# Attention and a mixture of experts on one core: the split of the next block's first weight quarters is moved ahead of its rows' transpositions

## The chip, the core and the metric

The kernel runs on one core of a Trainium2 chip. The core has five engines, each with an instruction queue of its own: TensorE (PE in the profile, with its weight loads shown as PEld), VectorE (DVE), ScalarE (ACT), GpSimd (POOL) and SyncE (SP), which here mostly starts DMA transfers. Engines meet only through semaphores. The metric is device time of one execution in microseconds (us). Lower is better.

## The reference, cut to what matters

```python
# attention: B, H, S, D = 8, 8, 576, 64, rotary embedding on q and k
scores = scale * np.matmul(q_rot, k_rot.transpose(0, 1, 3, 2))
attn = softmax(scores)
x = np.matmul(attn, v)            # then reshaped to (4608, 512)
# mixture of experts: 8 experts, the best one for each token
logits = x @ w_gate + modality_bias[modality_id]
e_idx = np.argmax(logits, axis=1)
gate_w = softmax(logits)[arange, e_idx]
for e in range(8):
    mask = e_idx == e
    h = np.maximum(x[mask] @ w1[e], 0.0)              # 512 -> 1024
    out[mask] = gate_w[mask, None] * (h @ w2[e])      # 1024 -> 512
```

Every number is float32. The kernel keeps that precision by splitting an operand into a high part in a rounded format and a low part (the rest), and adding up three products: high by high, high by low and low by high.

## The kernel before

The first half of the program is attention, in 32 steps of one pair of heads each. As attention runs, tokens are routed: the rank of a token in its expert's list is worked out, and its number and gate weight are scattered into a table. The second half takes the table in blocks of 256 tokens that share one expert. The profiled execution runs 19 blocks: 8 whose plan is made after five of the eight batches, and 11 whose plan comes last.

A block `s` has these steps, written by the functions whose names begin with `m_`:

- `m_rows` (L736): GpSimd gathers the block's rows of x into a tile XG, 8 indirect transfers, two blocks ahead.
- `m_load1`, `m_load2` (L752, L757): SyncE loads the expert's two weight matrices in quarters of 512 KB into ST1 and ST2, one block ahead, and only where the expert changes from the block before.
- `m_split(0, g)`: quarter g of the first matrix: ScalarE copies ST1 to W1H (the high part, L274), then VectorE subtracts it from ST1 and writes W1L (the low part, L271).
- `m_tr` (L781) and `m_tre`: VectorE transposes the two halves of XG in place, in squares of 32; then for each half ScalarE writes the rows' high part and VectorE the low part. Both parts lie in a tile that the profile calls HL, so these rows read `HL<-XG`.
- `m_l1` (L801): TensorE's first product, 4 groups of 24 matmuls. The first three matmuls of a group take W1H with the rows' high part, W1H with the rows' low part, and W1L with the rows' high part.
- `m_l1e` (L809, L810): ScalarE and VectorE take a group's result out of PSUM with the relu, split in two parts.
- `m_split(1, g)`: the same split for quarter g of the second matrix (W2H, W2L).
- `m_l2` (L818, L821, L822): TensorE's second product for half t of the block, 24 matmuls; ScalarE scales the result into y, and GpSimd scatters y to the output.

`chain` writes this out for all blocks. While TensorE works on block `s`, the other engines prepare block `s + 1`: once the last group's relu of block `s` is written, they have the time of the two `m_l2` for that block's first split and transpositions.

Between these steps `one()` puts one step of a list that is left over from routing: 14 steps that route the last batch, 5 that scatter its table rows, and 7 rounds of the second plan's arithmetic. They are short instructions, mostly on VectorE: 6 steps in block 0, 10 in each of blocks 1 and 2, and none from block 3 on.

The order of the instructions on TensorE, ScalarE, VectorE and GpSimd is that of the program text, and each of these engines takes its instructions strictly in that order. SyncE's order in the expert part is chosen by a scheduler.

One thing differs in block 0: its first product and the first half of its second (`m_l2(0, 0)`, with its y on ScalarE) are written before `chain` begins, so y of that half stands ahead of everything that block 0 does for block 1.

Of the kernel before, what the change touches and what calls it, by code (L numbers as in the profile page):

```python
# [85 lines left out]
def tile_attention_moe(ctx: ExitStack, tc: tile.TileContext, qk, v, mod, wg, mb, w1, w2, rope, cf, ci, out):  # L86
# [619 lines left out]
    def m_plan(s):  # L706
        ph, i = slots[s]
        pl = PLB if ph else PLA
        ms[s] = dict(
            e=nc.sync.value_load(pl[0:1, 0, i:i + 1], min_val=0, max_val=E - 1),  # L710
            r=nc.sync.value_load(pl[0:1, 1, i:i + 1], min_val=0, max_val=(E + 1) * N - BLK),
            c=nc.sync.value_load(pl[0:1, 2, i:i + 1], min_val=0, max_val=1))

    def m_ix(s):
        d = ms[s]
        ix = d["ix"] = ixp.tile([P, 2, 2], I32, name="ix", tag="ix")
        i1 = nc.sync.dma_start(out=ix, in_=TAB[bass.ds(d["r"], BLK), :].rearrange("(p t) w -> p t w", t=2)).ins
        xi = d["xi"] = ixp.tile([P, 8, 2], I32, name="xi", tag="xi")
        i2 = nc.sync.dma_start(out=xi, in_=TAB[bass.ds(d["r"], BLK), :].rearrange("(q g) w -> q (g w)", g=8).unsqueeze(0).to_broadcast([4, 32, 16])).ins
        if not slots[s][0]:  # L720
            for i in (i1, i2):
                for b, x in placed:
                    if b >= NPL:
                        tc.declare_no_dep(i, x, reason="the first plan's blocks lie before the rows of later batches")
                    else:
                        tc.add_manual_dep(i, x.name, mybir.DependencyInfo(mybir.DependencyClass.Sync, mybir.DependencyReason.DATA),
                                          reason="the table's rows of the first plan's batches")
                taken.append(i)
# [16 lines left out]
    def m_rows(s):  # L745
        for t in range(2):
            for g in range(4):
                m_gather(s, t, g)

    def m_load1(s, g):  # L750
        d = ms[s]
        nc.sync.dma_start(out=ST1[:, :, g * 256:(g + 1) * 256],  # L752
                          in_=w1[bass.ds(d["e"], 1), :, g * 256:(g + 1) * 256].rearrange("o (c p) f -> p (o c) f", p=P), cond=d["c"])

    def m_load2(s, g):
        d = ms[s]
        nc.sync.dma_start(out=ST2[:, g * 2:g * 2 + 2, :],  # L757
                          in_=w2[bass.ds(d["e"], 1), g * 256:(g + 1) * 256, :].rearrange("o (c p) f -> p (o c) f", p=P), cond=d["c"])

    def m_hi(i, g):  # L760
        sl = slice(g * 256, (g + 1) * 256)
        if i == 0:
            acopy(W1[0][:, :, sl], ST1[:, :, sl])
        else:
            acopy(W2[0][:, g * 2:g * 2 + 2, :], ST2[:, g * 2:g * 2 + 2, :])

    def m_lo(i, g):
        sl = slice(g * 256, (g + 1) * 256)
        if i == 0:
            sub(W1[1][:, :, sl], ST1[:, :, sl], W1[0][:, :, sl].bitcast(F32))  # L770
        else:
            sl = slice(g * 2, g * 2 + 2)
            sub(W2[1][:, sl, :], ST2[:, sl, :], W2[0][:, sl, :].bitcast(F32))

    def m_split(i, g):
        m_hi(i, g)
        m_lo(i, g)

    def m_tr(s, t):
        x = XG[s % 2][:, t]  # L780
        nc.vector.transpose(x, x)  # L781

    def m_tre(s, t):
        x = XG[s % 2][:, t].rearrange("p g (c q) -> p c g q", q=32)
        oh, ol = (a[:, :, t * P:(t + 1) * P].rearrange("p c (q g) -> p c g q", g=4) for a in (XTH, XTL))
        acopy(oh, x)
        sub(ol, x, oh.bitcast(F32))
# [3 lines left out]
    def m_l1(s, g):  # L791
        d = ms[s]
        if g == 0:
            d["hh"], d["hl"] = HHL[s % 2]
        ps = bank("H").rearrange("p (c r) -> p c r", r=BLK)
        for i in range(2):
            f0 = (g * 2 + i) * P
            m = 0
            for c in range(4):
                for w, x in ((W1[0], XTH), (W1[0], XTL), (W1[1], XTH)):  # L800
                    l1_[s] = nc.tensor.matmul(ps[:, i, :], w[:, c, f0:f0 + P], x[:, c, :], start=(m == 0), stop=(m == 11)).ins  # L801
                    m += 1
        d["ps", g] = ps

    def m_l1e(s, g):
        d = ms[s]
        ps = d["ps", g]
        sl = slice(g * 2, g * 2 + 2)
        nc.scalar.activation(d["hh"][:, sl, :], ps, AF.Relu)  # L809
        nc.vector.scalar_tensor_tensor(d["hl"][:, sl, :], ps, 0.0, d["hh"][:, sl, :].bitcast(F32), op0=ALU.max, op1=ALU.subtract)  # L810

    def m_l2(s, t):
        d = ms[s]
        ps = bank("Y")
        m = 0
        for c in range(8):
            for hx, w in ((d["hh"], W2[0]), (d["hl"], W2[0]), (d["hh"], W2[1])):
                nc.tensor.matmul(ps, hx[:, c, t * P:(t + 1) * P], w[:, c, :], start=(m == 0), stop=(m == 23))  # L818
                m += 1
        y = yp.tile([P, DM], F32, name="y", tag="y")  # L820
        nc.scalar.activation(y, ps, AF.Copy, scale=d["ix"][:, t, 1:2].bitcast(F32))  # L821
        nc.gpsimd.indirect_dma_start(out=out, out_offset=bass.IndirectOffsetOnAxis(ap=d["ix"][:, t, 0:1], axis=0),  # L822
                                     in_=y, in_offset=None, bounds_check=N - 1, oob_is_err=False)
# [13 lines left out]
    def one():  # L837
        if late:
            f, *a = late.pop(0)
            f(*a)  # L840
# [20 lines left out]
    for n in range(NPAIR):  # L861
# [34 lines left out]
        if n % 4 == 3:  # L896
            K_("XO", xout, n // 4)
            g = route(n // 4)
            steps = [(next, g, None)] * (NRK - (n == z))
            scats = [(scatter, n // 4, j) for j in range(5)]  # L900
            if n == z:

                g = plan()
# [4 lines left out]
            if n == 4 * NPL - 1:  # L908
                g = plan0()
# [62 lines left out]
    def chain(lo, hi, begun):  # L972
        if not begun:
            for g in range(4):
                m_split(0, g)
            for t in range(2):
                m_tr(lo, t)
                m_tre(lo, t)
        for s in range(lo, hi):
            nxt = s + 1 < hi  # L980
            if nxt:
                if s + 2 < hi and (not begun or s > 0):
                    m_rows(s + 2)
                if s + 3 < hi and (not begun or s > 0):
                    if s + 3 not in ms:
                        m_plan(s + 3)
                    m_ix(s + 3)
                for g in range(4):
                    if not begun or s > 0:
                        m_load1(s + 1, g)  # L990
            if not begun or s > lo:
                for g in range(4):
                    m_split(1, g)
                    m_l1(s, g)
                    m_l1e(s, g)
                    one()
            if nxt:
                for t in range(2):
                    m_tr(s + 1, t)
                for t in range(2):  # L1000
                    m_tre(s + 1, t)
                    one()
                for g in range(4):
                    m_load2(s + 1, g)
            if not begun or s > lo:
                m_l2(s, 0)
            if nxt:
                m_split(0, 0)
                one()
                m_split(0, 1)  # L1010
                one()
            m_l2(s, 1)
            if nxt:
                m_split(0, 2)
                one()
                m_split(0, 3)
                one()

    ns = NA + NB_STATIC
    chain(0, ns, True)  # L1020
    order.close()
    tot = nc.values_load(TOT[0:1, 0:1], min_val=0, max_val=NB_MAX)  # L1022
    with tc.If(tot > NB_STATIC):
        prefetch(ns)
        chain(ns, NA + NB_MAX, False)
# [100 lines left out]
```

## Time and profile before

| | |
|---|---|
| median of 3 runs | 935.73 us (935.01 to 935.83) |
| the profiled execution | 935.48 us, of which the span from the first to the last instruction is 933.7 us |
| granted TensorE clock, mean | 0.998 |
| PE busy | 899.7 us, 96% of the span |
| DVE busy | 670.0 us, 72% |
| POOL busy | 664.9 us, 71% |
| ACT busy | 629.5 us, 67% |

The profile's busy times are sums over a program with two halves; the expert part takes the span from about 493 us to the end. "Releaser" or an arrow `<-` after an idle time names what the engine waited for. A row that ends in `x2` merges two instructions that followed each other, and its time is that of both. A block takes TensorE a little over 22 us.

### The profile page before, as it was taken

The page shows a single profiled execution, that of the slowest core. Times are in us where ns is not written, and L with a number is a line of the kernel's source. Part 1 is how long each engine was busy: PE and PEld are TensorE (multiplying, and loading weights), DVE is VectorE, ACT ScalarE, POOL GpSimd, SP SyncE. Part 2 cuts the span into 40 slices and gives each one's busy share as a digit, 9 for nine tenths or more (in the row PEclk, how much of TensorE's full clock was granted, in tenths as well). Part 3 has the DMA queues.
Part 4 walks back from the last instruction along what each step waited for, and adds up shares of the span by engine and source line. Part 5 has one row for each costly group of instructions (what it writes and reads, how often), then busy time and mean ns, then how long its engine had stood idle before and what let it go on. Part 6 is the DMA issues. An engine that isn't in the chain of part 4 may idle for free. (4 is left out here: it accounts for less than half of the span.)

```text
span 933.7 us, 24945 instructions
## 1 busy us (share of the span) xinstructions
PE 899.7 (96%) x9248; PEld 739.8 (79%) x9248; DVE 670.0 (72%) x1165; ACT 629.5 (67%) x1292; POOL 664.9 (71%) x498
## 2 busy tenths in 40 slices
PE   2999999999999999999999999999999999999996
PEld 2777777777777777777778888898889999999995
DVE  7577787777877778777886778666666666666661
ACT  2778787787878778787884665665555666665651
POOL 3988879898898988999933877776655666666400
PEclk9999999999999999999999999999999999999999
DMA  8856857677676775766752721117712511251100
GB/s 264 237 171 186 227 156 199 197 182 215 169 200 197 184 218 159 205 179 187 209 157 75 209 64 36 51 62 235 231 46 72 195 41 55 92 180 46 37 24 17
DMA packets 79292, 136.90 MB, mean 147 GB/s; under 512 B 28699, under 2 KB 50603, under 8 KB 78140
## 3 DMA queue, kind: packets, MB, share of 16 engines
q1 hardware_dynamic: 68460, 114.06, 43.5%
q0 software_dynamic: 9440, 19.46, 6.4%
q10 hardware_dynamic: 1264, 1.72, 0.6%
q8 instruction: 75, 1.23, 0.6%
q14 instruction: 53, 0.43, 0.2%
HBM read 140.59 MB, written 19.77 MB: 172 GB/s over the span
## 5 line engine op out<-in xcount | busy, mean ns | idle before, releaser
L330 ACT ACTIVATE P<-ps,mn 128x576 f32<-128x576 f32 x288 | 210.4, 737 | 91.2 <-DVE mn L323 91.0
L323 DVE TENSOR_REDUCE mn<-ps 128x1 f32<-128x576 f32 x288 | 204.0, 745 | 93.0 <-PE ps L314 52.7
L736 POOL DMA_INDIRECT XG<-X,iy x152 | 186.4, 1226 | 66.8 <-issue 49.7
L801 PE MATMUL psH<-HL,W1H 128*128 128x256 f32 x1152 | 204.1, 280 | 0.0
L314 PE MATMUL ps<-SW 64*128 64x288 f32 x960 | 166.8, 314 | 15.5 <-DMA SW<-HL 15.4
L801 PEld LDWEIGHTS psH<-HL,W1H 128*128 128x128 f32 x1152 | 177.3, 188 | 1.9 <-ACT W1H L274 0.5
L314 PE MATMUL ps<-HL 64*128 64x288 f32 x960 | 166.6, 313 | 0.9 <-ACT P L330 0.8
L801 PE MATMUL psH<-HL,W1L 128*128 128x256 f32 x576 | 161.6, 281 | 1.4 <-DVE W1L L271 1.4
L314 PEld LDWEIGHTS ps<-SW 64*128 64x128 f32 x960 | 134.9, 190 | 26.9 <-DMA SW<-HL 15.0
L314 PEld LDWEIGHTS ps<-HL 64*128 64x128 f32 x960 | 137.1, 190 | 22.2 <-issue 12.8
L271 DVE TENSOR_TENSOR W1L<-ST,W1H 128x1024 fp32r<-128x1024 f32 x76 | 90.2, 1223 | 80.2 <-ACT W1H L274 80.2
L392 PE MATMUL pa<-PH,V 128*64 128x320 f32 (+1 forms) x1024 | 138.3, 412 | 0.0
L822 POOL DMA_INDIRECT out_dram<-y,ix x38 | 40.5, 1067 | 126.1 <-ACT y L821 103.1
L818 PE MATMUL psY<-W2H,SW 128*128 128x512 f32 x304 | 121.2, 399 | 0.0
L818 PE MATMUL psY<-W2L,SW 128*128 128x512 f32 x304 | 119.8, 394 | 0.0
L336 PE MATMUL ps<-idf,P 64*128 64x64 f32 x2624 | 105.8, 230 | 7.3 <-ACT P L330 1.8
L336 PEld LDWEIGHTS ps<-idf,P 64*128 64x128 f32 x2624 | 92.9, 141 | 22.3 <-ACT PH L274 9.0
L801 PEld LDWEIGHTS psH<-HL,W1L 128*128 128x128 f32 x576 | 108.4, 188 | 1.8 <-DVE W1L L271 1.8
L291 POOL TENSOR_TENSOR HL<-ST,HL 128x1216 fp32r<-128x1216 f32 x31 | 86.1, 2776 | 32.7 <-ACT HL L274 32.5
L392 PEld LDWEIGHTS pa<-PH,V 128*64 128x64 f32 x1024 | 67.9, 136 | 48.4 <-issue 10.0
L368 DVE COPY PH<-ps 128x512 f32<-128x512 f32 (+1 forms) x160 | 96.1, 633 | 8.6 <-PE ps L336 8.0
L271 DVE TENSOR_TENSOR W2L<-ST,W2H 128x1024 fp32r<-128x1024 f32 x76 | 92.6, 1219 | 4.5 <-ACT W2H L274 4.4
(173 smaller groups left out, 1585.4 us busy)
## 6 DMA issues: line engine op xcount, KB each, us to landing
ST<-in_moe_w_dram SPq DMA_DIRECT2D x152, 512.0 KB
ST<-in_qk_dram SPq DMA_DIRECT2D x62, 608.0 KB
SW<-HL SPq DMA_DIRECT2D x124, 232.0 KB
V<-in_v_dram SPq DMA_DIRECT2D x32, 256.0 KB
X<-X SPq DMA_DIRECT2D x8, 1024.0 KB
XG<-X,iy POOLq DMA_INDIRECT x152, 3.2
V<-in_v_dram SPq DMA_DIRECT2D x64, 16.0 KB
X<-XT SPq DMA_DIRECT2D x16, 64.0 KB
```

The source lines that it names most:

```text
L271: nc.vector.tensor_tensor(o, a, b, op=ALU.subtract)
L291: e.tensor_tensor(d["HL"][:, 1, c], a, d["HL"][:, 0, c].bitcast(F32), op=ALU.subtract)
L314: free(nc.tensor.matmul(ps[:, g, 0:288], t[:, wq, q0:q0 + P], t[:, wk, k0:k0 + 288], start=(m == 0), stop=(m == len(L) - 1)), seen)
L323: lastmin[d["ring", u]] = nc.vector.tensor_reduce(mn, d["S", u][:, :, 0:288], op=ALU.min, axis=AX.XY).ins
L330: nc.scalar.activation(p.rearrange("p (a b) -> p a b", a=2), ps[:, :, 0:288], AF.Exp, bias=d.pop(("m", u)), scale=-1.0, accum_out=d["sum"] ...
L336: free(nc.tensor.transpose(ps[0][:, g, c:c + 64], src[r, k0:k0 + P], idf[r, r]), ps[1])
L368: mine.append((nc.vector.tensor_copy if g else acopy)(o, i).ins)
L392: i = nc.tensor.matmul(pa[hh * 64:hh * 64 + 64, 0:c1 - c0], d["V"][:, hh, kt, :], r, start=(kt == 0), stop=(kt == 4))
L736: inst = nc.gpsimd.indirect_dma_start(out=XG[s % 2][:, t, g, :], out_offset=None, in_=X.rearrange("n (i f) -> (n i) f", f=P)[0:rows], in_o ...
L801: l1_[s] = nc.tensor.matmul(ps[:, i, :], w[:, c, f0:f0 + P], x[:, c, :], start=(m == 0), stop=(m == 11)).ins
L818: nc.tensor.matmul(ps, hx[:, c, t * P:(t + 1) * P], w[:, c, :], start=(m == 0), stop=(m == 23))
L822: nc.gpsimd.indirect_dma_start(out=out, out_offset=bass.IndirectOffsetOnAxis(ap=d["ix"][:, t, 0:1], axis=0), in_=y, in_offset=None, bounds ...
```

## The change

In `chain`, the two calls of `m_split(0, 0)` and `m_split(0, 1)` for block `s + 1`, each with a `one()` behind it, move from between the two `m_l2` to ahead of the two `m_tr`.

```diff
             if nxt:
+                for g in range(2):
+                    m_split(0, g)
+                    one()
                 for t in range(2):
                     m_tr(s + 1, t)
                 for t in range(2):
                     m_tre(s + 1, t)
                     one()
                 for g in range(4):
                     m_load2(s + 1, g)
             if not begun or s > lo:
                 m_l2(s, 0)
-            if nxt:
-                m_split(0, 0)
-                one()
-                m_split(0, 1)
-                one()
             m_l2(s, 1)
             if nxt:
                 m_split(0, 2)
```

Nothing is added or removed, and TensorE's and GpSimd's orders stay as they are. On VectorE, at the end of block 0 (the `XG` and `W1L` here belong to block 1; `lg` to `vm` are the left-over routing steps), the order before is:

```order
L525 TENSOR_REDUCE of<-rk 128x5
L781 STREAM_TRANSPOSE XG_76<-XG_76 128x512 x2
L271 TENSOR_TENSOR HL_81<-XG_76,HL_81 128x4x4x32 x2
L481 TENSOR_REDUCE lg<-G 128x40
L483 TENSOR_REDUCE mx<-lg 128x5
L271 TENSOR_TENSOR W1L<-ST_73,W1H 128x4x256
L486 TENSOR_TENSOR dl<-lg,mx 128x40
L488 TENSOR_SCALAR vv<-dl 128x40
L489 TENSOR_TENSOR vv<-vv,CF 128x40
L271 TENSOR_TENSOR W1L<-ST_73,W1H 128x4x256
```

and in the changed kernel:

```order
L525 TENSOR_REDUCE of<-rk 128x5
L271 TENSOR_TENSOR W1L<-ST_73,W1H 128x4x256 x2
L481 TENSOR_REDUCE lg<-G 128x40
L483 TENSOR_REDUCE mx<-lg 128x5
L781 STREAM_TRANSPOSE XG_76<-XG_76 128x512 x2
L271 TENSOR_TENSOR HL_81<-XG_76,HL_81 128x4x4x32
L486 TENSOR_TENSOR dl<-lg,mx 128x40
L488 TENSOR_SCALAR vv<-dl 128x40
L489 TENSOR_TENSOR vv<-vv,CF 128x40
L271 TENSOR_TENSOR HL_81<-XG_76,HL_81 128x4x4x32
```

The two weight subtractions moved to the front, and the routing steps `lg` and `mx`, which follow the second of them, now stand ahead of the transpositions; `dl` to the second `vv` stand between the two row subtractions.

On ScalarE at the same place, from block 0's first y on, the order before is:

```order
L821 ACTIVATE y<-psY,ix 128x512
L274 ACTIVATE HL_81<-XG_76 128x4x4x32
L274 ACTIVATE G<-XT 64x2x4x4 x2
L274 ACTIVATE HL_81<-XG_76 128x4x4x32
L274 ACTIVATE W1H<-ST_73 128x4x256 x2
```

and in the changed kernel:

```order
L821 ACTIVATE y<-psY,ix 128x512
L274 ACTIVATE W1H<-ST_73 128x4x256
L274 ACTIVATE G<-XT 64x2x4x4 x2
L274 ACTIVATE W1H<-ST_73 128x4x256
L274 ACTIVATE HL_81<-XG_76 128x4x4x32 x2
```

The weight copies changed places with the row copies. The first y stands ahead of both.

On VectorE at the end of block 1 (the `XG` and `W1L` here belong to block 2), the order before is:

```order
L810 SCALAR_TENSOR_TENSOR HL_82<-psH,SW_84 128x512
L781 STREAM_TRANSPOSE XG_75<-XG_75 128x512 x2
L271 TENSOR_TENSOR HL_81<-XG_75,HL_81 128x4x4x32
L520 TENSOR_TENSOR rk<-rk,OH 128x40
L271 TENSOR_TENSOR HL_81<-XG_75,HL_81 128x4x4x32
L522 RECIPROCAL VAL<-ee 128x5
L271 TENSOR_TENSOR W1L<-ST_73,W1H 128x4x256
```

and in the changed kernel:

```order
L810 SCALAR_TENSOR_TENSOR HL_82<-psH,SW_84 128x512
L271 TENSOR_TENSOR W1L<-ST_73,W1H 128x4x256
L520 TENSOR_TENSOR rk<-rk,OH 128x40
L271 TENSOR_TENSOR W1L<-ST_73,W1H 128x4x256
L522 RECIPROCAL VAL<-ee 128x5
L781 STREAM_TRANSPOSE XG_75<-XG_75 128x512 x2
L271 TENSOR_TENSOR HL_81<-XG_75,HL_81 128x4x4x32
```

Here too the weight subtractions moved ahead of the transpositions, with two short routing steps between them.

SyncE's order changes as well, in blocks 3 and 4 only: the loads of the first two W1 quarters for a later block move ahead of a run of reads of the second plan, and the loads of the other two quarters behind more of these reads than before.

## Rows read from the trace of the kernel before

**Rows 1.** Busy time of the engines in one block's stretch (TensorE first).

```profile
587.00:610.00 23.00, 23.00 (x148) 20.74 (x147) 16.24 (x17) 13.51 (x16) 16.78 (x15) 1.00 0.17 52
```

**Rows 2.** Waits of TensorE: total us, times, longest.

```profile
PE psH L801 <- DVE W1L L271: 1.4, 2, 0.8
```

**Rows 3.** Timeline of TensorE, start of block 1: start us, us, instruction, idle before.

```profile
518.09 0.40 PE L801 MATMUL psH<-HL,W1H 128*128 128x256 f32 x2
519.15 0.39 PE L801 MATMUL psH<-HL,W1L 128*128 128x256 f32 x1 [0.67 <-DVE W1L L271]
```

**Rows 4.** Timeline of TensorE, end of block 1 and start of block 2.

```profile
541.70 0.40 PE L818 MATMUL psY<-W2L,SW 128*128 128x512 f32 x1
542.13 0.51 PE L801 MATMUL psH<-HL,W1H 128*128 128x256 f32 x2
543.39 0.39 PE L801 MATMUL psH<-HL,W1L 128*128 128x256 f32 x1 [0.75 <-DVE W1L L271]
```

**Rows 5.** Timeline of TensorE, start of block 3.

```profile
565.71 0.40 PE L801 MATMUL psH<-HL,W1H 128*128 128x256 f32 x2
565.95 0.28 PE L801 MATMUL psH<-HL,W1L 128*128 128x256 f32 x1
```

**Rows 6.** Timeline of ScalarE, end of block 0.

```profile
512.69 0.69 ACT L821 ACTIVATE y<-psY,ix 128x512 f32<-128x512 f32 x1 [3.64 <-PE psY L818]
513.27 1.11 ACT L274 ACTIVATE HL<-XG 128x512 fp32r<-128x512 f32 x1
514.18 0.47 ACT L274 ACTIVATE G<-XT 64x32 f32<-64x32 f32 x2
514.67 1.14 ACT L274 ACTIVATE HL<-XG 128x512 fp32r<-128x512 f32 x1
```

**Rows 7.** Timeline of VectorE, end of block 0.

```profile
510.17 1.29 DVE L781 STREAM_TRANSPOSE XG<-XG 128x512 f32<-128x512 f32 x2
...
516.86 0.87 DVE L481 TENSOR_REDUCE lg<-G 128x40 f32<-128x360 f32 x1
...
517.88 1.21 DVE L271 TENSOR_TENSOR W1L<-ST,W1H 128x1024 fp32r<-128x1024 f32 x1
519.01 0.19 DVE L486 TENSOR_TENSOR dl<-lg,mx 128x40 f32<-128x40 f32 x1
...
519.57 1.22 DVE L271 TENSOR_TENSOR W1L<-ST,W1H 128x1024 fp32r<-128x1024 f32 x1
```

**Rows 8.** Timeline of all engines, end of a later block and start of the next.

```profile
689.44 0.60 ACT L809 ACTIVATE SW<-psH 128x512 fp32r<-128x512 f32 x1 [1.27 <-PE psH L801]
...
690.68 1.29 DVE L781 STREAM_TRANSPOSE XG<-XG 128x512 f32<-128x512 f32 x2
...
692.62 2.09 DVE L271 TENSOR_TENSOR HL<-XG,HL 128x512 fp32r<-128x512 f32 x2 [0.65 <-ACT HL L274]
...
695.67 2.00 ACT L274 ACTIVATE W1H<-ST 128x1024 fp32r<-128x1024 f32 x2
...
696.75 2.36 DVE L271 TENSOR_TENSOR W1L<-ST,W1H 128x1024 fp32r<-128x1024 f32 x2 [2.04 <-ACT W1H L274]
...
700.43 0.40 PE L801 MATMUL psH<-HL,W1H 128*128 128x256 f32 x2
```

**Rows 9.** Timeline of VectorE, end of block 1.

```profile
538.76 0.71 DVE L781 STREAM_TRANSPOSE XG<-XG 128x512 f32<-128x512 f32 x1 [4.11 <-DMA XG<-X,iy]
...
542.11 1.23 DVE L271 TENSOR_TENSOR W1L<-ST,W1H 128x1024 fp32r<-128x1024 f32 x1 [0.19 <-ACT W1H L274]
```

**Rows 10.** Timeline of VectorE, end of block 2.

```profile
556.71 1.30 DVE L781 STREAM_TRANSPOSE XG<-XG 128x512 f32<-128x512 f32 x2
...
564.23 1.22 DVE L271 TENSOR_TENSOR W1L<-ST,W1H 128x1024 fp32r<-128x1024 f32 x1
```

**Rows 11.** Timeline of TensorE, attention's first steps.

```profile
26.78 0.44 PE L314 MATMUL ps<-HL 64*128 64x288 f32 x1
...
35.31 0.29 PE L314 MATMUL ps<-SW 64*128 64x288 f32 x1
```

## The prediction

> **What bounds the kernel now.** I read first the busy times by stretch, then TensorE's waits, then TensorE's timeline at each place where one block ends and the next begins, and last what VectorE and ScalarE do there. In a stretch of one block TensorE is busy for all of 23.00 us, VectorE for 16.24 and ScalarE for 13.51 [rows 1]. So the expert part is TensorE's, and the other engines count only where they hand it something late. In the expert part TensorE's list has one wait, for W1L, 1.4 us in two places [rows 2]. Both are at starts of a block's first product: block 1 [rows 3] and block 2 [rows 4]. Each is a little more in clock time than the row's idle figure. The third matmul of a block normally starts 0.24 us after the first (565.95 - 565.71, [rows 5]). In block 1 it starts at 519.15, with the first at 518.09, so it is 519.15 - 518.33 = 0.8 us late. In block 2 the last matmul of the block before starts at 541.70; matmuls of that product follow each other at about 0.23, so the first could start at 541.93 and the third at 542.17; it starts at 543.39, 1.2 us late. These 2.0 us are all that an earlier W1L can win.
>
> **What the change does in a block without routing steps.** No instruction is added, so only the order counts: what TensorE needs at the start of the next block is W1 quarter 0 and the rows' two parts, and the rows now come last. Before, the last relu starts at 689.44, the rows are complete at 692.62 + 2.09 = 694.7, and W1L quarter 0 is there half-way through the pair of 2.36 that starts at 696.75, at about 698.0; TensorE begins at 700.43 and takes W1L as its third matmul [rows 8]. After: the weight copy can start when the relu ends, 690.04; its subtraction follows 696.75 - 695.67 = 1.08 later, at 691.1; the pair takes about 2.3, to 693.4; the row subtractions begin 692.62 - 690.68 = 1.94 after the transpositions begin, at 695.3, and end 2.09 later at 697.4. TensorE wants the rows' low part with its second matmul, at 700.55. The slack is 3.1 us where it was 2.7 for W1L: nothing changes there. y of the first half stands behind the row copies in either order and its tile has room, so it is hidden. The quarters' loads on SyncE are released about 5 us earlier, and they are used a block later, so that is hidden too. In blocks 3 and 4 SyncE's reads of the second plan stand ahead of other loads; behind them come the second matrix's loads, which wait in any case for this block's subtractions, so I cost it at nothing, and a load late by more than the 3 us slack would be what it costs if that cover is gone.
>
> **End of block 0: a new wait.** Here ScalarE stands on y of the first half until 512.69 and is free at 513.27 [rows 6]. Before, VectorE's transpositions ran inside that wait, at 510.17 [rows 7], and ScalarE's first work behind y was the rows. Now VectorE's first instruction is a weight subtraction, which must wait for a weight copy behind that y, and everything else queues behind it:
> - weight copy 0 starts at 513.27, its subtraction 1.08 later (the step from rows 8) at 514.35;
> - the two G copies hold ScalarE 514.67 - 514.18 = 0.49, after a copy's 0.91 to 0.95 (513.27 to 514.18), so weight copy 1 starts at 514.7 and its subtraction at 515.8. A subtraction holds VectorE 519.01 - 517.88 = 1.13, to 516.9;
> - `lg` and `mx` take 517.88 - 516.86 = 1.02, to 517.95;
> - the transpositions start there, the first row subtraction 1.94 later (rows 8) at 519.9, and it holds VectorE about 1.0 (half of 2.09), to 520.9;
> - `dl` and the two `vv` take 519.57 - 519.01 = 0.56, to 521.45;
> - the second row subtraction takes 1.1, to 522.5.
>
> So TensorE's second matmul of block 1 starts at about 522.6 and the third at 522.7 in place of 519.15 [rows 3]. That is 3.6 us later than before, with the old wait for W1L inside it. What TensorE then does is the same, and all of block 1's other work follows TensorE's relu steps, so the rest moves by 3.6 as a whole.
>
> **End of block 1: an old wait goes.** In the new time TensorE is ready for block 2 at 541.93 + 3.6 = 545.5. What holds the rows before is a gather that GpSimd issued earlier: the second transposition waits 4.11 for it, to 538.76, and the W1L subtraction that stands behind the rows starts at 542.11 [rows 9], so by the gather the rows are complete at about 542. By the other bound, the chain of a plain block, they are complete 697.4 - 689.44 = 8.0 after the last relu starts, and TensorE comes 700.43 - 689.44 = 11.0 after it [rows 8]; two short routing steps in between take some 0.5. The slack is over 2 us on either count, and W1L was done long before. So the 1.2 us of lateness at 543.39 goes.
>
> **End of block 2: close.** VectorE's work from the transpositions at 556.71 to the end of the second weight subtraction, 564.23 + 1.22 = 565.45, is one set of instructions, and the change permutes it: the row subtraction now ends it [rows 10]. TensorE wants that at 565.71 + 0.12 = 565.83 [rows 5]. I take 0; the bounds are 0 and 0.5 lost, if an extra handover falls in between.
>
> **The sum.** 3.6 - 1.2 = 2.4 us on the profiled execution's 935.48, so 937.9; the median of the runs shown is 0.25 higher, so 938.1. I count a difference of over 0.2% (1.9 us) as what a measurement of this kernel can tell from no change; the forecast is just beyond it.
>
> **What no row prices: TensorE's clock after the new stop.** TensorE would stand still from about 518.2 to 522.6, but for a matmul or two. Its stops in the expert part before are under 1 us [rows 3, 4], and the block behind them still runs at 0.28 a matmul [rows 5]. In attention's start the 288-column matmuls take 0.44 at 26.78 and 0.29 at 35.31 [rows 11]: the slow one of its two levels and the fast one (1.2 and 2.4 GHz), although the profile's granted clock reads 1.00 in both. So a stop could cost from 0 to, if the slow level lasted those 8.5 us at half rate, 4.3 us. I take 0 for the likeliest, because every stop seen after the start kept the fast level, and keep both ends.
> The Trainium skill, "TensorE: Matmul & The Clock Gate", section "Why this matters for your kernels", says that an idle gap of TensorE between bursts puts its clock back to half rate. No stop in this trace is long enough to show it; by that rule the clock rival below would be the result.
>
> **The rivals.**
> 1. The clock falls at the new stop. For it: the stop is several times any other in this part, and the slow level exists in this trace. Against it: no fall is seen after the start. With 2 us, the middle of 0 and 4.3, it gives 940.1.
> 2. The old waits go and no new one comes, which is faster: 935.73 - 2.0 = 933.7. The place is the same, end of block 0. It decides at 518.2, when TensorE wants the rows' low part: if the rows are complete by then, the change wins. For it: in each plain block the order has 3 us of slack. Against it: y at 512.69 stands ahead of all, and the steps behind it add up to 522.5, 4.3 us too late.
> 3. The new wait is real but small, or more comes back later, so that no change can be told: the wait would have to be under 3.1 us in place of 3.6 (1.9 + 1.2), as if the routing steps between the rows cost VectorE nothing (1.02 + 0.56 less gives a sum of 0.8). That gives 936.5. It is also where a change that does little ends up.
>
> **How the numbers follow.** The forecast has 0.57, with a range of its own of 937.3 to 938.9 (0.3 less or 0.5 more of VectorE's handovers, 0.5 at block 2). The clock has 0.20, the small wait 0.16, the faster rival 0.07. Of the forecast's chance about 0.50 lies beyond the 1.9 us and 0.07 within it; with the clock that is 0.70 slower, with the small wait 0.23 the same, and 0.07 faster. The range from 935.6 to 941.2 leaves out the faster rival and the upper half of the clock's price, together under 0.2.
>
> **What would show it.** In the changed kernel's timeline the transpositions for block 1 should start near 518 and not 510, the second row subtraction should end near 522.5, and TensorE's row at the start of block 1 should show a wait of some 1.7 to 4.4 us, named for the rows (HL) and not for W1L. No wait for W1L should be left. At the start of block 2 the wait should be gone, and the shift of TensorE against before should be 2.4 us from there to the end. A matmul of block 1 at twice the 0.12 step would show the clock. If the shift at block 1 is under 3 us, my steps on VectorE are wrong; if it changes after block 3, it is SyncE's order or a gather that I costed at nothing.

## The result, and the profile after

The changed kernel takes 940.19 us (median of 6 runs, 938.34 to 941.30), the kernel before 935.37 us (6 runs). The ratio is 1.0042, 95% interval 1.0027 to 1.0057: slower by 3.9 us (2.5 to 5.3) by the ratio; the two medians lie 4.8 apart. Run again, on one chip beside other kernels, it took 939.00 us against 935.71, ratio 1.0042 again (1.0026 to 1.0058). The forecast was 938.1 and slower.

The profiled execution took 940.92 us with a span of 939.0, which is 5.3 more than before. Of this only a part belongs to the change: block 0's last matmul already starts 1.7 us later (519.57 against 517.86), behind an attention part whose instructions are the same in both. Over the twelve profiled executions of this study that start lies anywhere between 516.7 and 520.0. So below I compare traces by the **tail**: from the start of block 0's last matmul to the end of the span. It is 933.7 - 517.86 = 415.8 before and 939.0 - 519.57 = 419.4 after, 3.6 more.

TensorE's list of waits in the changed kernel has no W1L any more, and two waits for the rows, in place of [rows 2] (columns: total us, times, longest):

```profile
PE psH L801 <- ACT HL L274: 2.7, 1, 2.7
PE psH L801 <- DVE HL L271: 1.4, 1, 1.4
```

Its timeline from the end of block 0 on answers to [rows 3]:

```profile
519.57 0.40 PE L818 MATMUL psY<-W2L,SW 128*128 128x512 f32 x1
522.62 0.39 PE L801 MATMUL psH<-HL,W1H 128*128 128x256 f32 x1 [2.65 <-ACT HL L274]
524.42 0.58 PE L801 MATMUL psH<-HL,W1H 128*128 128x256 f32 x1 [1.42 <-DVE HL L271]
524.80 0.41 PE L801 MATMUL psH<-HL,W1L 128*128 128x256 f32 x1
...
525.44 0.41 PE L801 MATMUL psH<-HL,W1L 128*128 128x256 f32 x1
...
527.36 0.41 PE L801 MATMUL psH<-HL,W1L 128*128 128x256 f32 x1
...
527.90 0.28 PE L801 MATMUL psH<-HL,W1L 128*128 128x256 f32 x1
...
528.26 0.28 PE L801 MATMUL psH<-HL,W1L 128*128 128x256 f32 x1
```

Two things stand in these rows. TensorE stops for 2.65 us, does one matmul, and stops for 1.42 more. And behind the second stop three matmuls take 0.64 (525.44 - 524.80) until about 527.6, and 0.36 from there on (528.26 - 527.90): the slow one of TensorE's two levels, 1.2 GHz, for some 3 us. The busy times by stretch show that too. The sixth figure behind the stretch's own length (the counts in brackets left out) is the granted clock, 1.00 before (first row) and 0.93 in the changed kernel:

```profile
517.00:541.00 24.00, 23.33 (x152) 20.85 (x151) 16.72 (x29) 12.27 (x17) 19.32 (x18) 1.00 0.79 212
517.00:541.00 24.00, 19.93 (x130) 18.14 (x129) 18.49 (x31) 13.23 (x18) 19.62 (x18) 0.93 0.72 189
```

ScalarE at the end of block 0, which answers to [rows 6], has the weights where the rows were, behind the same y:

```profile
514.40 0.69 ACT L821 ACTIVATE y<-psY,ix 128x512 f32<-128x512 f32 x1 [3.66 <-PE psY L818]
514.98 1.05 ACT L274 ACTIVATE W1H<-ST 128x1024 fp32r<-128x1024 f32 x1
...
520.52 2.04 ACT L274 ACTIVATE HL<-XG 128x512 fp32r<-128x512 f32 x2 [3.05 <-issue]
```

And VectorE, which answers to [rows 7]:

```profile
516.07 1.23 DVE L271 TENSOR_TENSOR W1L<-ST,W1H 128x1024 fp32r<-128x1024 f32 x1 [4.13 <-ACT W1H L274]
517.50 1.22 DVE L271 TENSOR_TENSOR W1L<-ST,W1H 128x1024 fp32r<-128x1024 f32 x1 [0.21 <-ACT W1H L274]
...
519.73 1.30 DVE L781 STREAM_TRANSPOSE XG<-XG 128x512 f32<-128x512 f32 x2
521.66 1.11 DVE L271 TENSOR_TENSOR HL<-XG,HL 128x512 fp32r<-128x512 f32 x1 [0.63 <-ACT HL L274]
...
523.27 1.10 DVE L271 TENSOR_TENSOR HL<-XG,HL 128x512 fp32r<-128x512 f32 x1
```

VectorE idles 4.13 us for the weight copy behind y; before, it transposed in that time. The transpositions start at 519.73, which is 518.0 in before's time, and the second row subtraction ends at 524.37, or 522.7. At the start of block 2 there is no wait any more, against [rows 4]; the last row is the start of block 3, against [rows 5]:

```profile
548.51 0.39 PE L818 MATMUL psY<-W2L,SW 128*128 128x512 f32 x1
548.74 0.40 PE L801 MATMUL psH<-HL,W1H 128*128 128x256 f32 x2
548.98 0.28 PE L801 MATMUL psH<-HL,W1L 128*128 128x256 f32 x1
...
571.20 0.40 PE L801 MATMUL psH<-HL,W1H 128*128 128x256 f32 x2
```

The account by the trace has three parts:

- The stop: the second matmul starts 4.85 us behind block 0's last one (524.42 - 519.57), so at the fast level the third would start at 4.97; before it started at 1.29 (519.15 - 517.86). That is 3.7 more, with the old wait of block 1 inside it.
- The slow stretch: from the third matmul to the start of block 2 it is 23.94 us (548.74 - 524.80), where before it was 22.78 to the time at which block 2 could have started (541.93 - 519.15), and the step from the second matmul to the third is 0.38 in place of 0.12. That is 1.4 more.
- The old wait of block 2: 1.2 less.

That sums to 3.9. Block 3 starts 51.6 us behind block 0's last matmul (571.20 - 519.57), against 47.9 before (565.71 - 517.86), which is 3.8 more. From there to the end it is 367.8 us, against 368.0 before, so nothing more is lost in the later blocks.

### The profile page after: what moved, and what is told of

It reads as the page before. It is cut to its first block, busy times and chain, and to the rows that moved or that the text cites. A ratio compares the mean times of both kernels' runs of the same rounds, so it can differ in the third digit from the quotient of the medians.

```text
span 939.0 us, 24928 instructions
## 1 busy us (share of the span) xinstructions
PE 900.9 (96%) x9248; PEld 741.4 (79%) x9248; DVE 670.1 (71%) x1165; ACT 625.0 (67%) x1292; POOL 669.6 (71%) x498
## 5 line engine op out<-in xcount | busy, mean ns | idle before, releaser
L736 POOL DMA_INDIRECT XG<-X,iy x152 | 182.9, 1203 | 66.7 <-issue 50.0
L822 POOL DMA_INDIRECT out_dram<-y,ix x38 | 46.6, 1226 | 125.4 <-ACT y L821 110.3
```

The source lines that it names most:

```text
L736: inst = nc.gpsimd.indirect_dma_start(out=XG[s % 2][:, t, g, :], out_offset=None, in_=X.rearrange("n (i f) -> (n i) f", f=P)[0:rows], in_o ...
```

## The experiments

The theory (A): the whole loss is made at one place, the end of block 0. There block 0's first y stands on ScalarE ahead of the weight copies; VectorE, whose queue now begins with a weight subtraction, idles behind it, and the rows come too late. The stop also drops TensorE's clock. The rivals: later blocks or SyncE's new order cost something; the weight split ahead of the rows costs by itself; the slow stretch has a cause other than the stop.

| kernel | median us | before beside it | ratio (95% interval) | tail against before |
|---|---|---|---|---|
| the change | 940.19 | 935.37 | 1.0042 (1.0027 to 1.0057) | +3.6 |
| the change again | 939.00 | 935.71 | 1.0042 (1.0026 to 1.0058) | +3.7 |
| in block 0 alone | 941.00 | 935.90 | 1.0056 (1.0037 to 1.0075) | +3.9 |
| in all blocks but 0 | 934.47 | 935.90 | 0.9981 (0.9968 to 0.9993) | -1.4 |
| routing steps behind the rows | 937.65 | 935.90 | 1.0021 (1.0006 to 1.0035) | 0.0 |
| first y behind the rows | 933.19 | 935.90 | 0.9973 (0.9962 to 0.9984) | -2.1 |
| the stop filled | 937.99 | 935.71 | 1.0023 (1.0011 to 1.0035) | +2.3 |
| before, first y behind the rows | 937.30 | 935.71 | 1.0021 (1.0001 to 1.0040) | +0.6 |

**In block 0 alone.** The new order is used at `s == 0`, the old one behind it.

```diff
-                for g in range(2):
-                    m_split(0, g)
-                    one()
+                if s == 0:
+                    for g in range(2):
+                        m_split(0, g)
+                        one()
...
+            if nxt and not (s == 0):
+                for g in range(2):
+                    m_split(0, g)
+                    one()
             m_l2(s, 1)
```

> The change is made at the end of block 0 alone; blocks 1 to 17 keep the old order. Theory A (the whole loss is made at the end of block 0: a new stop of TensorE of about 4.4 us, a stretch at its slow clock behind it, and the old wait of block 2 gone because TensorE comes later): the same as the whole change, 4 to 5 us slower than before, and TensorE's row at the start of block 1 waits for HL as there. Theory B (a part of the loss comes from the later blocks, by SyncE's new order or by transfers): at least 1 us less loss than the whole change, 2 to 3.5 us slower than before.

It is 1.0056 times before, no better than the whole change, with the same stop and the same slow matmuls:

```profile
518.23 0.40 PE L818 MATMUL psY<-W2L,SW 128*128 128x512 f32 x1
521.26 0.39 PE L801 MATMUL psH<-HL,W1H 128*128 128x256 f32 x1 [2.64 <-ACT HL L274]
523.09 0.43 PE L801 MATMUL psH<-HL,W1H 128*128 128x256 f32 x1 [1.44 <-DVE HL L271]
523.32 0.41 PE L801 MATMUL psH<-HL,W1L 128*128 128x256 f32 x1
```

So theory A holds for the loss. It tells one thing more: in this kernel block 2 has the old order, and its wait for W1L is gone too. TensorE's lateness alone is enough to make it go.

**In all blocks but 0.** The condition is turned round, `s > 0`.

> The change is made at the ends of blocks 1 to 17; block 0 keeps the old order. Theory A: the 0.8 us of lateness at block 1 stays, the 1.2 us at block 2 go, no new wait: 1.2 us faster than before (0.7 to 1.5). Theory B: 1 to 2 us slower than before, with a wait or a shift of TensorE behind block 2.

It is faster than before, ratio 0.9981 with an interval that leaves out 1. The wait at block 1 stays, that at block 2 is gone with TensorE on time:

```profile
517.04 0.40 PE L801 MATMUL psH<-HL,W1H 128*128 128x256 f32 x2
518.18 0.38 PE L801 MATMUL psH<-HL,W1L 128*128 128x256 f32 x1 [0.74 <-DVE W1L L271]
...
540.91 0.40 PE L801 MATMUL psH<-HL,W1H 128*128 128x256 f32 x2
541.14 0.28 PE L801 MATMUL psH<-HL,W1L 128*128 128x256 f32 x1
```

So the moved split alone is enough too to make the wait at block 2 go; in the whole change both hold. In these blocks the change does what it can: 1.2 us were forecast, the tail is 1.4 shorter. No loss comes from the later blocks.

**Routing steps behind the rows.** The four steps between block 0's splits and rows are written behind the rows.

```diff
                 for g in range(2):
                     m_split(0, g)
-                    one()
+                    if s > 0:
+                        one()
...
                     m_tre(s + 1, t)
-                    one()
+                    if s > 0:
+                        one()
+                if s == 0:
+                    for _ in range(4):
+                        one()
```

> The whole change, but the four routing steps that stand between the splits and the rows of block 1 are written behind the rows. Theory A (VectorE's row of instructions behind the first y sets the stop): lg, mx and dl to vv leave that row, 1.6 us, so the second matmul of block 1 starts 1.6 us earlier relative to the first y; the loss falls to 0.8 us without a slow stretch and to about 2.2 us with one. Rival (only the wait for y counts, the routing steps cost nothing): no gain over the whole change, 4 to 5 us slower than before.

The stop shrinks from 2.65 and 1.42 to 1.27 and 0.80, which is 2.0 us, of which 1.6 were forecast, and this execution has no slow matmul (three in a row take 521.42 - 521.07 = 0.35):

```profile
519.66 0.39 PE L801 MATMUL psH<-HL,W1H 128*128 128x256 f32 x1 [1.27 <-ACT HL L274]
520.85 0.39 PE L801 MATMUL psH<-HL,W1H 128*128 128x256 f32 x1 [0.80 <-DVE HL L271]
521.07 0.28 PE L801 MATMUL psH<-HL,W1L 128*128 128x256 f32 x1
...
521.42 0.28 PE L801 MATMUL psH<-HL,W1L 128*128 128x256 f32 x1
```

But the timed runs are at 1.0021, 2 us slower than before, where the tail is as long as before. Three more executions of the same kernel, each with its trace, were to settle that.

> The kernel with the routing steps behind the rows, looked at again: its first trace shows two short stops at block 1 (1.3 and 0.8 us) and no slow matmul, and by it the kernel should be 0.2 us slower than before, but its timed runs are 1.8 us slower, with a granted clock between 0.996 and 0.998. Theory A (stops of this size make TensorE slow in some executions and not in others): of three more traces at least one shows matmuls of block 1 at 0.21 in place of 0.12 for some us, and a granted clock of 0.996. Rival (the difference is spread over attention, where executions of one kernel differ by over 1 us anyway): none of the three shows it.

> As the look before it: one more execution of the same kernel, to see whether the slow stretch behind the short stops comes and goes (theory A) or never comes (rival).

> As the two looks before it: one more execution of the same kernel.

The three took 934.83, 936.48 and 937.66 us. All have the same two stops, 1.3 and 0.8. The first shows no slow matmul; the other two do, here the second:

```profile
518.62 0.39 PE L801 MATMUL psH<-HL,W1H 128*128 128x256 f32 x1 [1.27 <-ACT HL L274]
519.83 0.58 PE L801 MATMUL psH<-HL,W1H 128*128 128x256 f32 x1 [0.82 <-DVE HL L271]
520.20 0.42 PE L801 MATMUL psH<-HL,W1L 128*128 128x256 f32 x1
...
520.85 0.41 PE L801 MATMUL psH<-HL,W1L 128*128 128x256 f32 x1
```

From block 0's last matmul to block 3's first it is 48.0 and 48.3 us in the two executions without, 49.7 and 49.6 in the two with. Before, it is 47.9. So stops of this size cost the clock in some executions and not in others, and about 1.5 us when they do. That goes a good part of the way from the one trace to the median: of the twelve timed runs, the five with a granted clock of 0.996 have a median of 938.43 us, the seven with 0.997 or 0.998 one of 936.33.

**First y behind the rows.** `m_l2` is cut in two: the matmuls stay, and scaling and scatter of block 0's first half (`m_y(0, 0)`) come behind block 1's rows.

```diff
+        d["psy", t] = ps
+        if (s, t) != (0, 0):
+            m_y(s, t)
+
+    def m_y(s, t):
...
                     m_tre(s + 1, t)
                     one()
+                if s == 0:
+                    m_y(0, 0)
```

> The whole change, but the first y of block 0 (ScalarE's scaling and GpSimd's scatter) is written behind the split and the rows of block 1. Theory A (what makes the change lose is that this y stands ahead of ScalarE's weight copies): ScalarE copies the weights from about 2 us after the last relu, the rows are ready at 518.4 in before's time, the stop of TensorE is at most 0.3 us, no slow stretch, and both old waits are gone: 1.7 to 2.0 us faster than before. Rival (the weight split ahead of the rows costs by itself): the stop stays over 2 us and the kernel is at least 1 us slower than before.

It is the fastest kernel of the study, 933.19 us, ratio 0.9973. VectorE's first weight subtraction starts right behind `of`, as ScalarE no longer stands on y, and TensorE goes from block to block without a wait in its list (0.2 us of lateness remain at the third matmul, 518.79 - 518.34 - 0.24):

```profile
518.34 0.61 PE L801 MATMUL psH<-HL,W1H 128*128 128x256 f32 x2
518.79 0.28 PE L801 MATMUL psH<-HL,W1L 128*128 128x256 f32 x1
```

```profile
510.31 0.18 DVE L525 TENSOR_REDUCE of<-rk 128x5 f32<-128x40 f32 x1
510.41 2.52 DVE L271 TENSOR_TENSOR W1L<-ST,W1H 128x1024 fp32r<-128x1024 f32 x2
```

The split ahead of the rows costs nothing by itself: one instruction ahead of it did. The routing steps are where they are in the whole change, so by themselves they cost nothing either.

**The stop filled.** 17 matmuls on data of block 0, into a tile that nobody reads, stand between block 0's and block 1's products. They add work that the reference doesn't ask for.

```diff
             m_l2(s, 1)
+            if s == 0:
+                ps = bank("Y")
+                for _ in range(17):
+                    nc.tensor.matmul(ps, ms[0]["hh"][:, 0, 0:P], W2[0][:, 0, :], start=True, stop=True)
```

> The whole change, and 17 matmuls of 512 columns on block 0's own data into a PSUM tile that nobody reads, put between block 0's last matmul and block 1's first: about 17 x 0.233 = 4.0 us of TensorE work inside the stop of 4.4 us. Theory A (the stop itself makes TensorE run at its slow level for some 3 us behind it, which costs about 1.4 us beside the stop): the first product of block 1 runs at 0.12 a matmul from the start, block 1's third matmul starts where it did, and the kernel is 1.2 to 1.5 us faster than the whole change, about 2.5 us slower than before. Rival (the slow stretch has another cause, such as the load on memory at that place): the matmuls of block 1 stay at 0.21 a matmul and the time is that of the whole change, 4 to 5 us slower than before.

```profile
520.26 4.13 PE L1014 MATMUL psY<-W2H,SW 128*128 128x512 f32 x17
524.23 0.27 PE L801 MATMUL psH<-HL,W1H 128*128 128x256 f32 x1
524.92 0.39 PE L801 MATMUL psH<-HL,W1H 128*128 128x256 f32 x1 [0.41 <-DVE HL L271]
525.14 0.28 PE L801 MATMUL psH<-HL,W1L 128*128 128x256 f32 x1
...
525.49 0.28 PE L801 MATMUL psH<-HL,W1L 128*128 128x256 f32 x1
```

The rows come as late as in the change (second matmul 4.89 us behind block 0's last one at 520.03, against 4.85), but three matmuls take 0.35 at once. The timed runs agree on the clock: the granted clock is 0.994 to 0.996 in all 20 runs of the two kernels with the long stop (the change and the one in block 0 alone), and 0.997 or 0.998 in 11 of the 12 runs with the stop filled. So the idle stop is the cause of the slow stretch. What the stretch is worth is less sharp. The tail is 2.3 longer than before, where the change's is 3.6 and 3.7, so by the traces 1.3 to 1.4 us. The ratios, 1.0023 against 1.0042, say 1.8 us and the medians 1.0, with intervals that meet: the times alone do not show that the filled kernel is faster than the change.

**Before, first y behind the rows.** The old order, with only y moved by the same edit.

> The order of before, and only the first y of block 0 (with its scatter) written behind block 1's rows. Theory A (that y alone made W1L late for block 1, and the gather that GpSimd could not start before that y's scatter made the rows of block 2 late): both old waits go without any split being moved, 1.5 to 2.0 us faster than before, like the whole change with the y moved. Rival (the order of splits and rows is what makes W1L late for block 2): only the 0.8 us at block 1 go, the wait for W1L at block 2 stays, 0.8 us faster than before.

Both old waits went, as theory A said, and the kernel is no faster than before (ratio 1.0021, from 1.0001): a new wait comes at block 4, where neither theory had one.

```profile
518.58 0.40 PE L801 MATMUL psH<-HL,W1H 128*128 128x256 f32 x2
518.81 0.28 PE L801 MATMUL psH<-HL,W1L 128*128 128x256 f32 x1
...
588.13 0.51 PE L801 MATMUL psH<-HL,W1H 128*128 128x256 f32 x2 [1.63 <-ACT W1H L274]
589.39 0.39 PE L801 MATMUL psH<-HL,W1L 128*128 128x256 f32 x1 [0.76 <-DVE W1L L271]
```

ScalarE shows why. Block 3's first y waits for its buffer, which an earlier scatter still holds, and the weight copies stand behind it:

```profile
586.44 0.69 ACT L828 ACTIVATE y<-psY,ix 128x512 f32<-128x512 f32 x1 [5.27 <-DMA out_dram<-y,ix]
587.03 1.99 ACT L274 ACTIVATE W1H<-ST 128x1024 fp32r<-128x1024 f32 x2
```

The trace of before has a shorter wait of that kind at the same place, and TensorE does not feel it there:

```profile
583.77 0.69 ACT L821 ACTIVATE y<-psY,ix 128x512 f32<-128x512 f32 x1 [2.50 <-DMA out_dram<-y,ix]
```

The kernel with y moved and the splits ahead has waits of that kind too, 6.1 us on ScalarE in block 3, and TensorE doesn't feel them, since the copies stand ahead of y there:

```profile
575.69 2.00 ACT L274 ACTIVATE W1H<-ST 128x1024 fp32r<-128x1024 f32 x2
...
585.20 0.69 ACT L828 ACTIVATE y<-psY,ix 128x512 f32<-128x512 f32 x1 [3.29 <-DMA out_dram<-y,ix]
```

This is a worth of the moved split that TensorE's waits in the trace of before did not show: it takes the next block's weights out from behind a y that can be late. Why the scatters hold the buffer longer once y is moved stays open.

Up to block 3 this execution gains 2.3 us on before, and at block 4 it loses 2.9, so its tail is 0.6 longer. That does not account for the whole of the median. In six of the twelve timed runs the granted clock is 0.994 or 0.995, and these have a median of 939.2 us; the other six have 0.997 or 0.998 and a median of 936.2. The trace is of one of the latter, so where the clock fell in the others is not shown.

**The change again.**

> The changed kernel once more, beside the other two and the kernel before on one chip, to set the size of the loss: by the trace (3.6 us of stop more, 1.4 us of slow matmuls, 1.2 us of an old wait less) 3.8 us slower than before; by the first comparison 4.8 us. In every run the stop at block 1 and the slow stretch should be there.

The stop (2.65 and 1.42) and the slow stretch are there again, the tail is 3.7 longer, the ratio the same.

## Why the prediction was right, and which term was off

- **The direction and the place** were right, and so were the steps behind them. The new wait at the end of block 0 was worked out to put TensorE's second matmul at 522.6; it is at 524.42 - 1.7 = 522.7. The second row subtraction was to end at 522.5 and ends at 522.7, the transpositions were to start near 518 and start at 518.0. The kernel with y moved shows that y is what the row hangs on.
- **The size** was too small: 2.4 us forecast, 3.6 to 3.9 by the tails and ratios. Both medians lie above the forecast's own range of 937.3 to 938.9; they lie in the full range, to 941.2, because that one held half of the clock's price. That the time came out inside is owed to this rival and not to the sum. The step that failed is "I take 0 for the likeliest, because every stop seen after the start kept the fast level": the clock did fall, in all three executions with the long stop that have a trace, the one with the change in block 0 alone among them, and by their granted clock (0.994 to 0.996, before 0.996 to 0.998) in all timed runs of these kernels. It costs about 1.4 us, where I took 2 of the span from 0 to 4.3. So the first rival happened, at a chance of 0.20, and its 940.1 is the nearer one to the first median, 940.19 (the second, 939.00, lies between it and the forecast's 938.1). The argument was weak where it went from stops under 1 us to one of over 4. The Trainium skill, "TensorE: Matmul & The Clock Gate", section "Why this matters for your kernels", whose rule I set beside it, says that an idle gap of TensorE between bursts of matmuls puts its clock back to the slow level. The trace agrees that it falls (0.64 for three matmuls behind the stop, 0.36 some 3 us later). Each of the two stops, 2.65 and 1.42 us, is shorter than the gaps that the page warns of, and the clock fell all the same; here the measurement decides.
- **The old wait at block 2** went, 1.2 us as forecast. The reason given, that TensorE comes later than the rows and W1L, holds, but it is one of two: the moved split makes the wait go with TensorE on time as well.
- **Rival 2** (both waits go, nothing new) was right about what the order could do, and named the point that decides: with y out of the way it comes true, 933.19 against the 933.7 that I gave it.
- **Rival 3** made the routing steps its case. Taken out of the row they shorten the stop by 2.0, and the loss is no more than the 0.8 that it said (tails 0.0 and +0.5) in the two traced executions in which the clock stays up. The step is right, but the clock makes the median 2 us.
- **Costed at nothing** and found so: SyncE's new order and the earlier loads (the change in block 0 alone loses as much as the whole, and from block 3 on the time is that of before), and block 2's end (block 3 starts without a wait).
- **A reading that did not hold**: the tile of y was said to have room. At block 3 of the trace of before ScalarE waits 2.50 us for it (583.77). TensorE does not feel that wait, so the sum stands, but with the old order and y moved the same wait grew to 5.27 and cost TensorE 2.4 us at block 4.

## What to carry to other kernels

Before work is moved to the front of an in-order engine's queue, look at what already stands there at each end of the loop: here the first round was written differently, and one instruction that waits there stops all that is now behind it. When a change lets the bounding engine stop for longer than any stop in the trace, price the clock as a term, not as a rival. And judge an order by what can be late in it, not only by what is: the split ahead of y gains 1.2 us where TensorE is on time, and is what keeps the kernel fast once other waits are gone (tail -2.1 with it, +0.6 without).

## What the runs showed of the hardware that was not expected

- TensorE's clock fell behind two stops of 1.27 and 0.80 us with one matmul between them, in two of four executions of the same program, and behind stops of 2.65 and 1.42 us in each of the three that have a trace. The slow stretch lasted about 3 us each time. A pair of 1.63 and 0.76 us, in the one trace of the old order with y moved, left the clock up.
- The slow stretch costs about 1.3 to 1.5 us beside the stop by the traces, and 4 us of matmuls without use in place of the stop avoided it.
- The granted clock by stretch did show it, 0.93 over 24 us, where the slow matmuls of attention's start had read 1.00. In the trace of the kernel with y moved that start reads 0.51 (24 to 31 us), so a 1.00 there does not say that the clock was up.
